# Streaming 128 columns instead of 32 through the products of a triangular inverse

## The chip, the cores and the metric

The kernel runs on one core of a Trainium2 chip. The metric is the device time of one execution in microseconds. Engines are named as the profile names them: PE (TensorE matmuls), PEld (TensorE weight loads), DVE (VectorE), ACT (ScalarE), POOL (GpSimd) and SP (SyncE).

## The reference

Two blocks follow each other. The first is a recurrence over 768 steps, for 4 batch elements and 8 heads of width 40. Its output, regrouped as 3072 rows of 320, goes to a router that sends each row to one of 8 experts (320 to 1024 to 320), all in fp32.

```python
for t in range(S):
    y[:, :, t] = np.einsum('bhd,bhde->bhe', rt, state)
    Sa = np.einsum('bhde,bhe->bhd', state, at)
    state_decay = state * wt[:, :, None, :] - np.einsum('bhd,bhe->bhde', Sa, bt)
    state = state_decay + np.einsum('bhd,bhe->bhde', vt, kt)
...
expert_idx = np.argmax(logits, axis=1)
for e in range(E):
    h = np.maximum(x[mask] @ w1[e], 0.0)
    out[mask] = gate_w[mask, None] * (h @ w2[e])
```

## The kernel before

The recurrence is done in chunks of 32 steps. A tile holds four chunks of one batch element on the 128 partitions, for all 8 heads side by side; there are 24 tiles (6 tiles of 128 steps by 4 batch elements). For each chunk and head the kernel needs the inverse of a 32x32 triangular matrix. Because a tile has four chunks on 128 partitions, the matrices between steps are 128x128 and block diagonal, and one matmul per head handles four chunks at once.

Two functions share the work of a tile. `prepare` (line 192) does everything that needs no state, in parts divided by `yield`; `advance` (line 322) takes the four chunks one after the other through the state. The main loop (lines 447 to 454) traces `advance` of tile g and, at each of its yields, two parts of `prepare` of tile g+1. So the inverse of the next tile lies in the code between the chunks of this one. The order in which each engine gets its instructions is then set by the framework's scheduler, which reorders traced instructions by priority and by its own costs, allots buffers, and puts in all semaphores; that is why the rows below show PE's groups interleaved more finely than the code.

The steps of `prepare` that matter, in order:

- the products of decays (DVE scans at lines 202 and 205) and four sets of transposes on PE (line 237: `ln`, `an`, `kn`, `bn`, 40 rows by 40 columns each);
- `between` (line 242): the products `ne`, `ge`, `fe` (line 248), 40 rows deep, 128 columns streamed, evacuated with a mask by DVE (line 251);
- the inverse. It grows from blocks of 1 step to blocks of 32. The first level needs no product (line 292); the four others (lines 294 to 305) each do, for all 8 heads: transpose the present inverse `xt` in blocks on DVE (`turned`, line 281), spread it into the block diagonal `xe` on POOL (line 270), multiply `w = ne' xt` on PE (line 298), copy it to `ws` on ACT (line 300), multiply `x = xe' ws` on PE (line 303), and write part of the result into `xt` under a mask on DVE (line 304). `xt` and `ws` hold 8 heads of 32 columns, so a matmul streams 32 columns for one head;
- `te`, the block diagonal of the inverse (line 270 from line 306), then `gv` (line 312, 40 columns streamed) and `pt` (line 321, 128 rows deep, 128 columns streamed, 40 columns of weights).

`advance` has the first products of the tile (`u_ps` at line 332 and `y_ps` at line 337), per chunk the small matmuls at lines 349, 357, 362, 374 and 378 (32 or 40 rows deep, 40 columns) with DVE's updates of the state, and behind the chunks `ut` (387), `he` (248), `y_ps` (391), the row's logits (`lg_ps`, 408) and its gate. An fp32 matmul stands in the trace as two passes, each with a weight load of its own, so 8 heads make 16 passes. The transposes at line 237 are one pass each.

PSUM has eight banks; the pool `mmp` (line 99) gives five of them in turn to everything that asks for `bank(...)`: `w_ps` and `x_ps` take one each at every level. Three more hold `u`, `y` and `s`.

After the recurrence, some 2200 us into the span, the rows are sorted by expert and the experts run (lines 573 to 675): matmuls 128 rows deep that stream 512 (line 618) and 320 columns (line 645).

Of the kernel before, what the change touches and what calls it, by code (L numbers as in the profile page):

```python
# [14 lines left out]
AX = mybir.AxisListType  # L15
PSUM = bass.MemoryType.PSUM
CMAGIC = 12582912.0
# keeps a square root's argument in range; its root is lost in the 1e-6 that is added
TINY = 1e-30
P = 128  # L20
L = 32
# [3 lines left out]
def bc(ap, shape, axis):  # L25
    return ap.unsqueeze(axis).to_broadcast(shape)
# [3 lines left out]
def kernel(  # L30
# [12 lines left out]
    moe_w2: bass.AP,  # L43
    out: bass.AP,
):
    """RWKV-7 state recurrence in chunks of L steps, then top-1 routed experts.

    With lam_t the product of a chunk's decays before step t, per channel e,
        at = a lam_t,  kt = k / lam_(t+1),  bt = b / lam_(t+1)
        U  = (I + tril(at bt'))^-1 (at S' + tril(at kt') V)  # L50
        y  = lam (r S + tril(r V') kt - tril(r U') bt)
        S <- (S + V' kt - U' bt) lam_L
    where S is the state at the chunk's start and tril is strict.  A tile holds four chunks of
    one batch element on 128 partitions, so that matrices between steps are block diagonal.
    The kernel carries -U.  The inverse grows from blocks of one step to blocks of L steps:
    the off-diagonal block of a pair of inverted blocks X is that of X N X.
    """
    nc = tc.nc
    B, NT, D, H, _ = rT.shape
    S = NT * P  # L60
    N = B * S
# [33 lines left out]
    with ExitStack() as attn:  # L95
        cst = attn.enter_context(tc.tile_pool(name="cst", bufs=1))
        one = attn.enter_context(tc.tile_pool(name="one", bufs=1))
        two = attn.enter_context(tc.tile_pool(name="two", bufs=2))
# [3 lines left out]
        def bank(name):  # L102
            return mmp.tile([P, 512], FP32, tag="mm", name=name)

# [1 line left out]
        blk = cst.tile([P, P], FP32, name="blk")  # L106
        nc.vector.memset(blk, 0.0)
        for c in range(NCK):
# [28 lines left out]
        for j in range(L.bit_length() - 1):  # L137
            m = cst.tile([P, L], I32, name=f"level{j}")
# [7 lines left out]
        first = cst.tile([D, W1C], FP32, name="first")  # L146
# [2 lines left out]
        decay = cst.tile([D, W1C], FP32, name="decay")  # L149
        nc.vector.memset(decay[:, 0 :: L + 1], 0.0)  # L150

# [1 line left out]
        emb = two.tile([P, XW], FP32, tag="xr", name="emb")[0:E, 0:DM]  # L153
        nc.sync.dma_start(out=emb, in_=moe_expert_emb)
        tau = cst.tile([E, 1], FP32, name="tau")
# [15 lines left out]
        def h3(t):  # L171
            return t[:, 0:DM].rearrange("p (h d) -> p h d", h=H)

        def half(t):
            return t.rearrange("p (h x) -> p h x", h=4)

        state = {}
# [12 lines left out]
            loaded[g] = d  # L190

        def prepare(g, d):
            """Everything of a tile that needs no state, in parts."""
            d.update(loaded.pop(g))
            ck = "p (x t) -> p x t"

            # products of decays: before a step, and after it to the chunk's end
            body = decay[:, 0 : W1C - 1].rearrange(ck, t=L + 1)
            nc.scalar.copy(body[:, :, 1:], d["w"].rearrange("p h (c t) -> p (h c) t", t=L))
            lam = one.tile([D, W1C], FP32, tag="lam", name="lam")  # L200
            suf = one.tile([D, W1C], FP32, tag="suf", name="suf")
            nc.vector.tensor_tensor_scan(
                lam, decay, first, initial=0.0, op0=ALU.mult, op1=ALU.add
# [26 lines left out]
            nc.gpsimd.tensor_tensor(d["k"], d["k"], d["w"], ALU.mult)  # L230
            nc.gpsimd.tensor_tensor(d["b"], d["b"], d["w"], ALU.mult)

            # steps on partitions
            for nm, src in (("ln", lx), ("an", d["a"]), ("kn", d["k"]), ("bn", d["b"])):
                ps = h3(bank(f"{nm}_ps"))
                for h in range(H):
# [5 lines left out]
            def between(nm, lhs, rhs, mask, pool):  # L242
                t = pool.tile([P, H, P], FP32, tag=nm, name=nm)
                for q in range(2):
                    ps = half(bank(f"{nm}_ps"))
                    for j in range(4):
                        h = 4 * q + j
                        nc.tensor.matmul(  # L248
                            ps[:, j], lhsT=lhs[:, h], rhs=rhs[:, h], start=True, stop=True
                        )  # L250
                    nc.vector.tensor_tensor(
                        t[:, 4 * q : 4 * q + 4], ps, bc(mask, [P, 4, P], 1), ALU.mult
                    )
                return t

            d["between"] = between
            ne = between("ne", d["a"], d["b"], nlower, one)
# [7 lines left out]
            def c3(t):  # L265
                return t[:, 0 : H * L].rearrange("p (h j) -> p h j", h=H)

            def block_diagonal(x, nm):
                t = one.tile([P, H, P], FP32, tag=nm, name=nm)
                nc.gpsimd.tensor_tensor(  # L270
                    t.rearrange("p h (c j) -> p h c j", c=NCK),
                    bc(x, [P, H, NCK, L], 2),
                    bc(blk.rearrange("p (c j) -> p c j", c=NCK), [P, H, NCK, L], 1),
                    ALU.mult,
                )
                return t

            # inverse of I - N, transposed
            def turned(x):
                t = two.tile([P, H, L], FP32, tag="xn", name="xn")  # L280
                nc.vector.transpose(  # L281
                    t.rearrange("p h j -> p (h j)"), x.rearrange("p h j -> p (h j)")
                )
                return t

            xt = two.tile([P, H, L], FP32, tag="xt", name="xt")
# [6 lines left out]
            yield  # L293
            for m in levels[1:]:
                xe = block_diagonal(turned(xt), "xe")
                ps = c3(bank("w_ps"))
                for h in range(H):
                    nc.tensor.matmul(ps[:, h], lhsT=ne[:, h], rhs=xt[:, h], start=True, stop=True)  # L298
                ws = two.tile([P, H, L], FP32, tag="ws", name="ws")
                nc.scalar.copy(ws, ps)  # L300
                ps = c3(bank("x_ps"))
                for h in range(H):
                    nc.tensor.matmul(ps[:, h], lhsT=xe[:, h], rhs=ws[:, h], start=True, stop=True)  # L303
                nc.vector.copy_predicated(xt, bc(m, [P, H, L], 1), ps)  # L304
                yield
            te = block_diagonal(xt, "te")

# [9 lines left out]
            for q in range(2):  # L317
                ps = half(bank("pt_ps"))
                for j in range(4):
                    h = 4 * q + j  # L320
# [3 lines left out]
                nc.scalar.copy(pt[:, 4 * q : 4 * q + 4], ps[0:D])  # L324

        def advance(g, d):
            """Four chunks through the state; the tile's rows of x, their gates and experts."""
            b, i = groups[g]
            u_ps = h3(acc.tile([P, 512], FP32, tag="u", name="u_ps"))
            y_ps = h3(acc.tile([P, 512], FP32, tag="y", name="y_ps"))  # L330
            for h in range(H):
                nc.tensor.matmul(
                    u_ps[:, h], lhsT=d["te"][:, h], rhs=d["gv"][:, h],
                    start=(h == 0), stop=False, skip_group_check=True,
                )
            for h in range(H):
                nc.tensor.matmul(
                    y_ps[:, h], lhsT=d["fe"][:, h], rhs=d["kn"][:, h],
                    start=(h == 0), stop=False, skip_group_check=True,
# [3 lines left out]
            for c in range(NCK):  # L343
                r0 = L * c
                rows = slice(r0, r0 + L)
                last = i == NT - 1 and c == NCK - 1
                st = state[b]
                for h in range(H):
                    nc.tensor.matmul(  # L349
                        u_ps[rows, h], lhsT=d["pt"][:, h, rows], rhs=st[:, h],  # L350
                        start=False, stop=True, skip_group_check=True,
                    )
                nc.vector.tensor_scalar(un[rows], u_ps[rows], -1.0, None, ALU.mult)
                if not last:
                    s_ps = h3(acc.tile([P, 512], FP32, tag="s", name="s_ps"))[0:D]
                    for h in range(H):
                        nc.tensor.matmul(  # L357
                            s_ps[:, h], lhsT=d["kn"][rows, h], rhs=d["vn"][rows, h],
                            start=(h == 0), stop=False, skip_group_check=True,
                        )  # L360
                    for h in range(H):
                        nc.tensor.matmul(  # L362
                            s_ps[:, h], lhsT=d["bn"][rows, h], rhs=un[rows, h],
                            start=False, stop=True, skip_group_check=True,
# [12 lines left out]
                for h in range(H):  # L377
                    nc.tensor.matmul(  # L378
                        y_ps[rows, h], lhsT=d["r"][:, h, rows], rhs=sn[:, h],
                        start=False, stop=False, skip_group_check=True,  # L380
# [3 lines left out]
            for q in range(2):  # L384
                ps = half(bank("ut_ps"))
# [4 lines left out]
            for h in range(H):  # L390
                nc.tensor.matmul(
                    y_ps[:, h], lhsT=he[:, h], rhs=d["bn"][:, h],
                    start=False, stop=True, skip_group_check=True,
                )
            xr = two.tile([P, XW], FP32, tag="xr", name="xr")
            x = xr[:, 0:DM]
            nc.vector.tensor_tensor(h3(xr), y_ps, d["ln"], ALU.mult)

            # logits times the row's norm, the first of the largest, the gate
            xt_ps = bank("xt_ps")  # L400
            for j, (k0, kn) in enumerate(KC):
                nc.tensor.transpose(xt_ps[0:kn, j * P : j * P + P], xr[:, k0 : k0 + kn], ident)
# [4 lines left out]
            for j, (_, kn) in enumerate(KC):  # L407
                nc.tensor.matmul(
                    lg_ps, lhsT=xs[0:kn, j], rhs=embT[0:kn, j],
                    start=(j == 0), stop=(j == len(KC) - 1),  # L410
# [34 lines left out]
        for _ in prepare(0, ready):  # L445
            pass
        for g in range(NG):
            now, ready = ready, {}
            ahead = prepare(g + 1, ready) if g + 1 < NG else iter(())
            for _ in advance(g, now):  # L450
                next(ahead, None)
                next(ahead, None)
            for _ in ahead:
                pass
            if g % 2 == 1 and g // 2 < E:
                load_w2(g // 2)
# [7 lines left out]
        )  # L464
        nc.scalar.dma_start(out=w1_sb[0 : KC[2][1], e, 2], in_=moe_w1[e, 2 * P : DM])

# [1 line left out]
    with ExitStack() as rt:  # L468
        rp = rt.enter_context(tc.tile_pool(name="rp", bufs=1))
        rps = rt.enter_context(tc.tile_pool(name="rps", bufs=1, space=PSUM))  # L470
# [15 lines left out]
        for e in range(1, E):  # L486
# [3 lines left out]
        before = rp.tile([P, P], FP32, name="before")  # L490
# [7 lines left out]
            rk, lhsT=ones, rhs=cumx.rearrange("p s e -> p (s e)"),  # L498
            start=True, stop=False, skip_group_check=True,
# [3 lines left out]
            start=False, stop=True, skip_group_check=True,  # L503
# [16 lines left out]
        off = rp.tile([P, E], FP32, name="off")  # L520
# [11 lines left out]
        nc.vector.scalar_tensor_tensor(  # L532
            out=lo, in0=bk, scalar=-float(P), in1=dest, op0=ALU.mult, op1=ALU.add
        )
        # tokens as two parts under 64, which bfloat16 holds exactly, as it does 0 and 1
        shp = [P, NSLOT, NBLK]
        bm = rp.tile(shp, FP32, name="bm")
        nc.vector.tensor_tensor(bm, bc(io_p[:, 0:NBLK], shp, 1), bc(bk, shp, 2), ALU.is_equal)
# [5 lines left out]
        q = NSLOT // 4  # L544
# [5 lines left out]
        for s in range(NSLOT):  # L550
            nc.tensor.matmul(
                inv, lhsT=oh[:, s], rhs=rr[:, s].rearrange("p t k -> p (t k)"),
                start=(s == 0), stop=(s == NSLOT - 1),
# [16 lines left out]
        nc.vector.tensor_reduce(n1.unsqueeze(2), cm, axis=AX.X, op=ALU.add)  # L570
        nc.vector.tensor_scalar(eblk, n1, -1.0, None, ALU.add)

# [1 line left out]
    fw = ctx.enter_context(tc.tile_pool(name="fw", bufs=2))  # L574
    xins = [fw.tile([P, XW], FP32, name=f"xin{j}", bufs=1) for j in range(XBUF)]
    for t in xins:
# [140 lines left out]
```

## Time and profile before

| | |
|---|---|
| runs | 2609.22 us and 8315.88 us |
| median of the two | 5462.55 us |
| span of the profiled execution | 2610.3 us |
| the run that agrees with that span | 2609.22 us |
| PE busy | 2519.8 us, 97% |
| PEld busy | 2211.9 us, 85% |
| DVE, ACT, POOL busy | 692.9, 375.9, 542.8 us |

The profile is of one execution. Busy time is the time in which an engine had an instruction in flight. Since matmuls are pipelined, a group of n passes is best priced by the start of the next group less its own start, over n: the mean ns that the table of lines gives for one pass includes the pass before it. The granted clock is TensorE's, as a share of full speed: 1.00 is 2.4 GHz and 0.50 is 1.2 GHz.

### The profile page before, as it was taken

What the parts mean: (1) busy time and instruction counts of PE and PEld (TensorE: products, weight loads), DVE (VectorE), ACT (ScalarE), POOL (GpSimd) and SP (SyncE); (2) the same over time, 40 slices, a digit from 0 to 9 for tenths busy, and PEclk for the clock granted to TensorE, in tenths of its full rate; (3) what the DMA queues carried; (4) which work ended last, traced back from release to release, by engine and by line L of the source; (5) the groups of instructions that cost most, each with busy time, mean ns of one, the idle gap of its engine ahead of it and who ended that gap; (6) DMA issues with size and microseconds to landing.
All of it is one profiled execution on the core that took longest, in us unless ns stands there. A gap on an engine that the chain in (4) does not pass through costs nothing. (4 is left out here: it accounts for less than half of the span.)

```text
span 2610.3 us, 35907 instructions
## 1 busy us (share of the span) xinstructions
PE 2519.8 (97%) x15728; PEld 2211.9 (85%) x15728; DVE 692.9 (27%) x1374; ACT 375.9 (14%) x769; POOL 542.8 (21%) x336
## 2 busy tenths in 40 slices
PE   6999999999999999999999999999999998699998
PEld 5999999999999999999999999999999997255554
DVE  4232232233223223312322331332233122211111
ACT  1011111011111101111110111111011102011111
POOL 3122212212211221221122122212211210211111
PEclk9655555555555555555555555555555555799999
DMA  6000000000000000000000000000000001400000
GB/s 199 11 21 9 16 19 13 14 16 21 9 16 19 12 15 16 21 9 16 19 13 14 16 21 9 16 19 13 13 19 19 6 4 33 155 26 28 23 21 6
DMA packets 28411, 62.65 MB, mean 24 GB/s; under 512 B 4052, under 2 KB 18398, under 8 KB 28256
## 3 DMA queue, kind: packets, MB, share of 16 engines
q1 hardware_dynamic: 16320, 39.88, 5.0%
q10 hardware_dynamic: 8960, 12.58, 1.6%
q0 software_dynamic: 2976, 7.89, 1.0%
q8 instruction: 126, 2.06, 0.3%
q14 instruction: 29, 0.24, 0.0%
HBM read 53.60 MB, written 9.02 MB: 24 GB/s over the span
## 5 line engine op out<-in xcount | busy, mean ns | idle before, releaser
L270 POOL TENSOR_TENSOR xe<-xn,blk 128x1024 f32<-128x1024 f32 x96 | 226.9, 2364 | 1194.9 <-DVE xn L281 1011.3
L298 PE MATMUL w_ps<-xt,ne 128*128 128x32 f32 x1536 | 352.4, 403 | 3.2 <-DVE xt L304 3.2
L303 PE MATMUL x_ps<-ws,xe 128*128 128x32 f32 x1536 | 346.9, 402 | 8.1 <-ACT ws L300 7.3
L303 PEld LDWEIGHTS x_ps<-ws,xe 128*128 128x128 f32 x1536 | 334.7, 330 | 16.8 <-issue 7.4
L298 PEld LDWEIGHTS w_ps<-xt,ne 128*128 128x128 f32 x1536 | 336.4, 329 | 13.8 <-DVE xt L304 4.0
L618 PE MATMUL h_ps<-w_sb,xT 128*128 x372 | 184.6, 622 | 8.0 <-DMA w_sb<-in_moe_w_dram 8.0
L618 PEld LDWEIGHTS h_ps<-w_sb,xT 128*128 128x128 f32 x372 | 63.1, 189 | 113.7 <-issue 109.1
L304 DVE COPY_PREDICATED xt<-level,x_ps 128x256 f32<-128x256 int32 x96 | 42.4, 442 | 418.3 <-PE x_ps L303 418.3
L357 PE MATMUL s_ps<-vn,kn 32*40 32x40 f32 x1472 | 142.6, 265 | 0.0
L367 DVE TENSOR_TENSOR st<-s_ps,st 40x320 f32<-40x320 f32 x92 | 44.4, 483 | 367.0 <-PE s_ps L362 367.0
L300 ACT COPY ws<-w_ps 128x256 f32<-128x256 f32 x96 | 35.7, 372 | 728.4 <-PE w_ps L298 728.4
L645 PE MATMUL y_ps<-w_sb,hT 128*128 x496 | 138.8, 433 | 0.0
L376 ACT COPY sn<-sn_ps 40x320 f32<-40x320 f32 x96 | 40.2, 419 | 613.7 <-PE sn_ps L374 613.7
L357 PEld LDWEIGHTS s_ps<-vn,kn 32*40 32x40 f32 x1472 | 112.3, 171 | 19.0 <-issue 5.4
L349 PE MATMUL u_ps<-st,pt 40*32 40x40 f32 x1536 | 125.9, 264 | 0.0
L378 PE MATMUL y_ps<-sn,in_r 40*32 40x40 f32 x1536 | 122.6, 265 | 0.0
L378 PEld LDWEIGHTS y_ps<-sn,in_r 40*32 40x32 f32 x1536 | 106.6, 163 | 17.7 <-issue 13.2
L645 PEld LDWEIGHTS y_ps<-w_sb,hT 128*128 128x128 f32 x496 | 91.7, 190 | 34.2
L349 PEld LDWEIGHTS u_ps<-st,pt 40*32 40x32 f32 x1536 | 106.9, 162 | 16.2 <-issue 9.4
L362 PE MATMUL s_ps<-un,bn 32*40 32x40 f32 x1472 | 116.9, 263 | 0.4 <-DVE gs L434 0.4
L362 PEld LDWEIGHTS s_ps<-un,bn 32*40 32x40 f32 x1472 | 105.9, 176 | 7.1 <-issue 4.5
L248 PE MATMUL fe_ps<-in_r,in_v 40*128 40x128 f32 x384 | 105.7, 444 | 0.0
(180 smaller groups left out, 3301.4 us busy)
## 6 DMA issues: line engine op xcount, KB each, us to landing
w_sb<-in_moe_w_dram ACTq DMA_DIRECT2D x8, 1280.0 KB
w_sb<-in_moe_w_dram SPq DMA_DIRECT2D x8, 1024.0 KB
x_rows<-xr SPq DMA_DIRECT2D x24, 160.5 KB
in_w<-in_wT_dram SPq DMA_DIRECT2D x24, 160.0 KB
in_a<-in_aT_dram SPq DMA_DIRECT2D x24, 160.0 KB
in_k<-in_kT_dram SPq DMA_DIRECT2D x24, 160.0 KB
in_b<-in_bT_dram SPq DMA_DIRECT2D x24, 160.0 KB
in_v<-in_vT_dram SPq DMA_DIRECT2D x24, 160.0 KB
```

Source lines behind the costliest of these rows:

```text
L248: nc.tensor.matmul(ps[:, j], lhsT=lhs[:, h], rhs=rhs[:, h], start=True, stop=True)
L270: nc.gpsimd.tensor_tensor(t.rearrange("p h (c j) -> p h c j", c=NCK), bc(x, [P, H, NCK, L], 2), bc(blk.rearrange("p (c j) -> p c j", c=NCK ...
L298: nc.tensor.matmul(ps[:, h], lhsT=ne[:, h], rhs=xt[:, h], start=True, stop=True)
L303: nc.tensor.matmul(ps[:, h], lhsT=xe[:, h], rhs=ws[:, h], start=True, stop=True)
L304: nc.vector.copy_predicated(xt, bc(m, [P, H, L], 1), ps)
L349: nc.tensor.matmul(u_ps[rows, h], lhsT=d["pt"][:, h, rows], rhs=st[:, h], start=False, stop=True, skip_group_check=True,)
L357: nc.tensor.matmul(s_ps[:, h], lhsT=d["kn"][rows, h], rhs=d["vn"][rows, h], start=(h == 0), stop=False, skip_group_check=True,)
L362: nc.tensor.matmul(s_ps[:, h], lhsT=d["bn"][rows, h], rhs=un[rows, h], start=False, stop=True, skip_group_check=True,)
L367: nc.vector.tensor_tensor(new, s_ps, st, ALU.add)
L378: nc.tensor.matmul(y_ps[rows, h], lhsT=d["r"][:, h, rows], rhs=sn[:, h], start=False, stop=False, skip_group_check=True,)
L618: nc.tensor.matmul(ps, lhsT=d["xT"][0:kn, c], rhs=w1f[0:kn, ds(ek * (len(KC) * F) + c * F + q * 512, 512)], start=(c == 0), stop=(c == len ...
L645: nc.tensor.matmul(ps, lhsT=d["hT"][:, c], rhs=w2f[:, ds(d["ek"] * (FC * DM) + c * DM, DM)], start=(c == 0), stop=(c == FC - 1),)
```

## The change

At each of the four levels that multiply, the 8 heads are taken in two groups of four. The streamed operand of each matmul is now the 32 columns of all four heads of the group (128 columns), for `w` and for `x`. A head's matmul gives the product of its own weights with all four heads' columns, fills a quarter of a bank, and of its 128 columns the 32 of its own head are kept. So a level has as many matmuls, weights and passes as before, each with four times the columns; it takes four PSUM banks in place of two; and the one ACT copy and the one masked DVE copy of 256 columns become eight of each with 32 columns, four behind each bank. The masks, the transposes, `xe` and the results are unchanged. Comments and the docstring are blanked, which leaves the line numbers ahead of the loop as they were.

```diff
             for m in levels[1:]:
                 xe = block_diagonal(turned(xt), "xe")
-                ps = c3(bank("w_ps"))
-                for h in range(H):
-                    nc.tensor.matmul(ps[:, h], lhsT=ne[:, h], rhs=xt[:, h], start=True, stop=True)
                 ws = two.tile([P, H, L], FP32, tag="ws", name="ws")
-                nc.scalar.copy(ws, ps)
-                ps = c3(bank("x_ps"))
-                for h in range(H):
-                    nc.tensor.matmul(ps[:, h], lhsT=xe[:, h], rhs=ws[:, h], start=True, stop=True)
-                nc.vector.copy_predicated(xt, bc(m, [P, H, L], 1), ps)
+                wide = "p (h x) -> p h x"
+                for q in range(2):
+                    ps = bank("w_ps")
+                    rhs = xt[:, 4 * q : 4 * q + 4].rearrange("p h j -> p (h j)")
+                    for j in range(4):
+                        nc.tensor.matmul(
+                            ps[:, P * j : P * j + P], lhsT=ne[:, 4 * q + j], rhs=rhs,
+                            start=True, stop=True,
+                        )
+                    for j in range(4):
+                        o = P * j + L * j
+                        nc.scalar.copy(ws[:, 4 * q + j], ps[:, o : o + L])
+                for q in range(2):
+                    ps = bank("x_ps")
+                    rhs = ws[:, 4 * q : 4 * q + 4].rearrange("p h j -> p (h j)")
+                    for j in range(4):
+                        nc.tensor.matmul(
+                            ps[:, P * j : P * j + P], lhsT=xe[:, 4 * q + j], rhs=rhs,
+                            start=True, stop=True,
+                        )
+                    for j in range(4):
+                        o = P * j + L * j
+                        nc.vector.copy_predicated(xt[:, 4 * q + j], m, ps[:, o : o + L])
                 yield
```

## Rows read from the trace of the kernel before

**Rows 1.** The page: span, busy times, granted clock in 40 equal slices.
```profile
span 2610.3 us, 35907 instructions
...
PE 2519.8 (97%) x15728; PEld 2211.9 (85%) x15728; DVE 692.9 (27%) x1374; ACT 375.9 (14%) x769; POOL 542.8 (21%) x336
...
PEclk9655555555555555555555555555555555799999
```

**Rows 2.** Stages: window, length, busy PE PEld DVE ACT POOL, clock, DMA share, GB/s.
```profile
300.00:1000.00 700.00, 693.78 (x4643) 648.55 (x4643) 192.87 (x366) 105.33 (x221) 152.69 (x79) 0.50 0.05 15
...
2300.00:2500.00 200.00, 200.00 (x681) 107.14 (x680) 33.54 (x86) 30.41 (x53) 35.82 (x35) 1.00 0.08 26
```

**Rows 3.** Groups of instructions by line and shape, whole span.
```profile
L298 PE MATMUL w_ps<-xt,ne 128*128 128x32 f32 x1536 | 352.4, 403 | 3.2 <-DVE xt L304 3.2
L303 PE MATMUL x_ps<-ws,xe 128*128 128x32 f32 x1536 | 346.9, 402 | 8.1 <-ACT ws L300 7.3 <-POOL xe L270 0.8
...
L270 POOL TENSOR_TENSOR xe<-xn,blk 128x1024 f32<-128x1024 f32 x96 | 226.9, 2364 | 1194.9 <-DVE xn L281 1011.3 <-DVE lam_l L210 183.6
...
L312 PE MATMUL gv_ps<-vn,ge 128*128 128x40 f32 x384 | 87.8, 415 | 0.0
```

**Rows 4.** Timeline of PE around one level: start us, us, engine, line, names, passes.
```profile
1001.36 3.62 PE L248 MATMUL ge_ps<-in_a,in_k 40*128 40x128 f32 x16
1004.90 0.74 PE L349 MATMUL u_ps<-st,pt 40*32 40x40 f32 x8
...
1013.85 1.27 PE L349 MATMUL u_ps<-st,pt 40*32 40x40 f32 x16
1015.06 0.35 PE L357 MATMUL s_ps<-vn,kn 32*40 32x40 f32 x2
...
1015.98 3.62 PE L298 MATMUL w_ps<-xt,ne 128*128 128x32 f32 x16
1019.53 1.28 PE L362 MATMUL s_ps<-un,bn 32*40 32x40 f32 x16
...
1021.95 3.62 PE L303 MATMUL x_ps<-ws,xe 128*128 128x32 f32 x16
```

**Rows 5.** Stretches of 2 us with a raised clock: window, length, PE busy, clock.
```profile
172.00:174.00 2.00, 2.00 (x21) 0.82 0.00 0
174.00:176.00 2.00, 2.00 (x33) 1.00 0.00 0
176.00:178.00 2.00, 2.00 (x12) 0.53 0.24 82
...
2176.00:2178.00 2.00, 2.00 (x27) 0.91 0.00 0
```

**Rows 6.** Timeline of PE where the clock rises, and of a tile without.
```profile
81.09 1.98 PE L332 MATMUL u_ps<-gv,te 128*128 128x40 f32 x16
83.00 0.69 PE L237 MATMUL ln_ps<-ident,lx 40*128 40x40 f32 x8
...
992.92 2.88 PE L321 MATMUL pt_ps<-te,an 128*40 128x128 f32 x14
995.73 0.68 PE L237 MATMUL ln_ps<-ident,lx 40*128 40x40 f32 x8
996.25 0.67 PE L237 MATMUL an_ps<-ident,in_a 40*128 40x40 f32 x8
...
1085.37 1.07 PE L237 MATMUL ln_ps<-ident,lx 40*128 40x40 f32 x8
1086.25 1.05 PE L237 MATMUL an_ps<-ident,in_a 40*128 40x40 f32 x8
```

**Rows 7.** Groups by line and shape: evacuations from PSUM.
```profile
L304 DVE COPY_PREDICATED xt<-level,x_ps 128x256 f32<-128x256 int32 x96 | 42.4, 442 | 418.3 <-PE x_ps L303 418.3
...
L300 ACT COPY ws<-w_ps 128x256 f32<-128x256 f32 x96 | 35.7, 372 | 728.4 <-PE w_ps L298 728.4
...
L314 ACT COPY gv<-gv_ps 128x320 f32<-128x320 f32 x24 | 10.2, 426 | 83.6 <-PE gv_ps L312 83.6
```

## The prediction

> **What bounds the kernel now.** I read the page first: TensorE is busy for 97% of the span, no other engine for more than 27%, and the line of granted clocks stands at 5 tenths from the third slice to the thirty-third [rows 1]. The table of stages says the same without rounding: from 300 to 1000 us PE is busy for 693.78 of 700 us at a clock of 0.50, which is the lower of its two levels, 1.2 GHz; the experts, from 2300 to 2500 us, run at 1.00, 2.4 GHz [rows 2]. So the recurrence, some 2200 us, is bound by PE, and by a PE at half speed. What a change is worth here is read in PE time, and a change of clock is worth more than anything that another engine can give.
>
> The groups by line come next [rows 3]. The two products of the inverse, lines 298 and 303, are its largest: 1536 passes each, 352.4 and 346.9 us, together 27% of the span. PE sits idle ahead of them for 3.2 and 8.1 us in all, so their inputs nearly always lie ready.
>
> Then the timeline, for the price of one pass [rows 4]. The 16 passes of `w` start at 1015.98 and the next group at 1019.53: 222 ns a pass for 32 streamed columns. The 16 passes of `ge` start at 1001.36 and the next group at 1004.90: 221 ns for 128 streamed columns. Both have weights of 128 columns. A small pass, 40 rows with weights of 32 columns and 40 streamed, takes 76 ns (1013.85 to 1015.06 for 16). So the weight load sets the pace of `w`, and the columns flow beside the next load: 96 more columns cost nothing in the nearest row. The Trainium skill ("TensorE: Matmul & The Clock Gate", section "Back-to-back issue gap") speaks against this: it gives the gap between single matmuls as the streamed columns over the clock, so that four times the columns would be four times the gap, 107 in place of 27 ns at the lower clock. By that alone the 3072 passes would grow by an estimated 3072 x 80 ns = 246 us; the two equal rows disagree with it for weights of this width.
>
> Last, where the clock rises within the recurrence. Stretches of 2 us show seven spells above 0.50, near 172, 630, 994, 1268, 1632, 2086 and 2176 us, of which the first and last stand in [rows 5]; each lasts about 3.4 us (in the first 0.82, 1.00 and 0.53, so 1.3, 2 and 0.1 us at the upper level). In each of them the engine had just done `pt`. In the third, 14 passes of it, 128 rows deep and 128 columns wide, run from 992.92 to 995.73, and the transposes behind them take 65 ns each (995.73 to 996.25 for 8), against 110 ns in a tile without the spell (1085.37 to 1086.25) [rows 6]. There is an eighth at 81 us behind the first tile's `pt`: `u_ps` takes 119 ns a pass there (81.09 to 83.00 for 16), though it has the same weights as the passes of 222 ns. (The recorded clock of 1.00 ahead of that is not borne out: passes have the slow pace until then.) So 8 of 24 stretches of `pt` raised the clock. Neither `ge` and its kin (128 columns, 40 rows deep) nor `gv` (128 rows, 40 columns streamed, [rows 3]), nor the present `w` and `x` (128 rows, 32 columns) was ever followed by a rise of its own. All the while PE was as good as always busy.
>
> **The change part by part.** *The passes.* As many as before, 2 x 1536, with the same weights. At the lower clock 128 columns cost between nothing (`ge`) and, if each pass were 10 ns longer because its stream is now as long as its load, 3072 x 10 ns = 31 us. I take 5 us, near `ge`. A gain is excluded, since the loads are the same.
>
> *The clock.* After the change every stretch of `w` or `x` is 16 passes, 128 rows deep and 128 columns wide: what `pt` is, but for weights of 128 columns in place of 40, and the experts, which hold 1.00, have such weights. There are 8 such stretches per tile (4 levels, `w` and `x`) where there was one of `pt`. If each raises the clock as often as `pt` did, that is 8/3 = 2.7 spells per tile. The bounds are none and one for each stretch, 8; most `pt` stretches are cut in two by the logits' passes and the `w` stretch in [rows 4] is whole, so I go a little up, to 3. The price of one spell of 3.4 us is bounded by two rows [rows 4, 6]: with transposes 3.4 x (110/65 - 1) = 2.35 us of work gained, with passes of 128 weight columns 3.4 x (222/119 - 1) = 2.9 us. What follows `w` is mostly small passes, nearer to the transposes: 2.3 us. Sum: 3 x 2.3 x 24 = 166 us.
>
> *The evacuations.* ACT's copy takes 372 ns for 256 columns and 426 ns for 320 [rows 7], so 0.84 ns a column and some 157 ns fixed: 184 ns for 32 columns. Eight take 1.47 us, 1.1 us more per level, 96 x 1.1 = 106 us on an engine that is busy for 375.9. The masked copy on DVE has only its 442 ns; with a like fixed part one of 32 columns takes some 0.2 us, eight 1.6 us, 111 us more on an engine busy for 692.9. Neither becomes the bound. What counts is the tail between a stretch of PE and the next. Four of the eight copies wait for the first bank alone and run beside the second half of the stretch; behind `w` four copies of 0.18 us stand in place of one of 0.37, and the first half of `x` needs only the earlier four. Behind `x` four masked copies, 0.8 us, stand in place of 0.44, and then come the transpose and POOL's 2.36 us [rows 3] as before. This tail has small matmuls of the present tile to hide it, at 1019.53 for one [rows 4]; it shows where there are none, in the first tile, and where PE gets ahead. Between nothing and 0.45 us at each of 96 levels, 43 us: I take 10.
>
> *The banks.* A level takes four of the five shared banks in turn in place of two. A bank is held longer only by its four short copies, and PE has 3.5 us of work in the other bank of the pair. I cost it at nothing; if the cover is gone, it is part of the 43 us above.
>
> The sum: 5 + 10 - 166 = -151 us. The profiled span of 2610.3 us agrees with the run of 2609.22; the median of 5462.55 is the midpoint of that run and one of 8315.88, a time that neither had and that nothing in the profile accounts for. The forecast is made against 2609.22: 2609 - 151 = 2458 us.
>
> **The rivals.** *The clock stays up through the levels.* If the scheduler puts `x` right behind `w`, or if a raised clock needs less to stay than to rise, the whole stretch of the levels, 1014 to 1058 of a tile's 90 us, runs at 1.00. At 119/222 and 65/110 of the pace that is 44 x 0.43 = 19 us per tile: 2609 - 24 x 19 + 15 = 2168. Against it: every spell seen ended after some 3.4 us, and at 2.4 GHz a stretch of 16 passes is over in 2 us.
>
> *The clock does not rise.* `gv`, as deep and with the same 128 weight columns, never raised it; perhaps the long load is what keeps `w` from it, not the columns. Then only the costs remain: 2609 + 15 = 2624. A rule of the Trainium skill leads there too (the same page, section "What's actually happening"): the clock is set by how busy PE has recently been. By it the recurrence, with PE 99% busy, would be at full clock already and wider streams could give nothing. The 0.50 beside 693.78 of 700 us disagrees with that plain reading.
>
> *The evacuations decide* (slower). If the copies do not overlap with the other half, and PE finds nothing else to do, a level gets longer by all that they add, 1.1 + 1.16 = 2.3 us, 217 us in 96 levels: 2609 + 217 + 5 - 166 = 2665. It decides from 166/96 = 1.7 us per level on. For it speaks that `x` already waits for `ws` in places (7.3 us, [rows 3]); against it, that those waits are 11 us in 192 stretches.
>
> *Load and stream in sequence* (slower). If a stream 128 rows deep does not fit beside the load, a pass gains what 128 columns take alone: some 222 ns of a `ge` pass less the 76 ns of a small one, 146 ns, or 449 us in all: 2609 + 449 - 166 = 2892. It decides from 166 us/3072 = 54 ns per pass on. `ge` speaks against it. The page's estimate of 246 us from above, put in its place, would give 2609 + 246 - 166 = 2689.
>
> **How the numbers follow.** The forecast has 0.72, the clock that stays up 0.10, the clock that does not rise 0.10, the evacuations 0.06, the sequence 0.02. Five spells per tile with the sum's costs make 2609 - 276 + 15 = 2348, two with both costs at their upper bound 2609 - 110 + 74 = 2573: that is the likeliest case's own range. Below I stop at 2340; above I reach to 2625, to take in the clock that does not rise. The other three cases, 0.18, are left out. Some 2% is what a measurement of this kernel can tell from no change, so faster means under 2557: 0.69 of the first case and all of the second, 0.79. Within 2% are 0.03 of the first and the third case, 0.13. Slower is 0.08.
>
> **What would show it.** Right: in stretches of 2 us, spells at 1.00 in the middle of the tiles, behind `w` or `x`, three or so per tile; groups of 16 passes with 128 columns that take 3.5 to 3.7 us at 0.50 and near 2 us at 1.00; the mean clock of 300 to 1000 us near 0.56 (3 x 3.4 of 84 us); PE still busy above 97%. Wrong: a clock of 0.50 throughout; passes of `w` above 235 ns at the lower clock; idle time of PE ahead of lines 298 and 303 in tens of us, released by ACT or DVE. If whole tiles stand at 1.00, the first rival was right.

## The result and the profile after

The changed kernel takes 2189.22 us (2181.05 and 2197.39), 0.8385 of the time before, with an interval of 0.8249 to 0.8522. Run again beside its experiments it took 2189.42 us against 2612.88, a ratio of 0.8354 (0.8317 to 0.8392); the ratios are taken over runs in the faster of two states, and one repeat of 2210.57 us was in the slower. So it is faster by a sixth, 420 us, where 151 us were forecast; the time of 2189 us lies below the range of 2340 to 2625 us. All ratios below are against the kernel before on the same chip, whose runs there lay between 2606 and 2618 us.

The page of the changed kernel, against [rows 1]: span, busy times, and the granted clock in 40 equal slices.

```profile
span 2195.7 us, 37553 instructions
...
PE 2063.8 (94%) x15728; PEld 1765.9 (80%) x15728; DVE 837.1 (38%) x2046; ACT 428.0 (19%) x1441; POOL 581.9 (26%) x336
...
PEclk9677656657776677766776577657666657999999
```

PE has the same 15728 passes and is busy for 456 us less; its share fell to 94%, where above 97% was expected, since it now waits (below). The clock line explains how: 6 and 7 tenths through the recurrence in place of 5 (0.70 from 300 to 1000 us, where 0.56 was forecast). DVE has 144 us more and ACT 52, neither near a bound.

The groups by line, against [rows 3, 7]; the change moves line 298 to 302, 303 to 313, 300 to 308 and 304 to 319, and what follows by 15.

```profile
L270 POOL TENSOR_TENSOR xe<-xn,blk 128x1024 f32<-128x1024 f32 x96 | 261.9, 2729 | 876.0 <-DVE xn L281 858.2 <-DVE lam_l L210 17.8
L302 PE MATMUL w_ps<-xt,ne 128*128 128x128 f32 x1536 | 258.0, 324 | 4.4 <-DVE xt L319 4.4
...
L313 PE MATMUL x_ps<-ws,xe 128*128 128x128 f32 x1536 | 221.6, 305 | 46.5 <-POOL xe L270 46.5
...
L383 DVE TENSOR_TENSOR st<-st,lam_l 40x320 f32<-40x320 f32 x92 | 113.5, 1234 | 2.3
...
L319 DVE COPY_PREDICATED xt<-level,x_ps 128x32 f32<-128x32 int32 x768 | 93.5, 189 | 263.0 <-PE x_ps L313 262.9
...
L308 ACT COPY ws<-w_ps 128x32 f32<-128x32 f32 x768 | 87.1, 200 | 359.9 <-PE w_ps L302 359.6
```

`w` and `x` with four times the columns take 480 us in place of 699. A small masked copy costs 189 ns (some 200 were forecast), a small ACT copy 200 (184 were); four in a row overlap, so each engine has 51 us more of them, half of what was forecast. New is PE's wait ahead of `x`, 46.5 us for POOL, where 8.1 us for ACT and POOL stood before.

One tile by stages, the changed kernel: transposes to the first `w`, the levels to the end of the last `x`, and the rest to the next tile's transposes.

```profile
1018.00:1038.60 20.60, 20.60 (x178) 18.94 (x177) 11.11 (x17) 4.44 (x10) 0.00 (x0) 0.56 0.14 41
1038.60:1065.80 27.20, 25.80 (x259) 24.07 (x257) 12.37 (x39) 4.46 (x34) 11.31 (x4) 0.83 0.01 2
1065.80:1088.80 23.00, 22.41 (x178) 20.50 (x177) 8.84 (x21) 6.97 (x14) 10.65 (x6) 0.70 0.08 22
```

The same three stages of a tile before:

```profile
995.70:1016.00 20.30, 20.30 (x178) 18.53 (x177) 11.28 (x17) 3.88 (x9) 0.00 (x0) 0.57 0.14 41
1016.00:1057.80 41.80, 41.61 (x297) 39.89 (x297) 6.88 (x17) 3.37 (x7) 13.59 (x6) 0.50 0.02 5
1057.80:1085.40 27.60, 27.02 (x139) 24.57 (x138) 7.27 (x15) 6.00 (x12) 6.07 (x4) 0.50 0.04 12
```

This is where the time went: the three stages of this tile are 18.9 us shorter, the levels by 14.6, at a clock of 0.83 in place of 0.50, and what follows them by 4.6, at 0.70 for 0.50 (the first is 0.3 longer). Stretches of 2 us (window, length, PE busy, clock) show one long spell in this tile, from the end of the first level's `x` into the passes behind `he`:

```profile
1046.00:1048.00 2.00, 2.00 (x12) 0.54 0.00 0
...
1050.00:1052.00 2.00, 1.33 (x27) 1.00 0.00 0
...
1062.00:1064.00 2.00, 1.26 (x25) 1.00 0.00 0
...
1074.00:1076.00 2.00, 2.00 (x18) 0.78 0.38 90
```

Nothing like the 3.4 us of [rows 5]: the clock is up from 1047.8 to 1075.1, 27.3 us. It outlasts stretches in which PE is idle for a third of the time. Over the recurrence there is one long spell per tile, of 17 to 27 us, and 17 short ones of 3.4 us as before, mostly behind `pt`; from 100 us on to the experts 628 us are spent at 1.00, where it was 24.

The timeline of PE in that spell (start, us, engine, line, names, passes, idle before and its releaser), against [rows 4]:

```profile
1043.70 1.70 PE L302 MATMUL w_ps<-xt,ne 128*128 128x128 f32 x7
1045.19 3.21 PE L313 MATMUL x_ps<-ws,xe 128*128 128x128 f32 x16
1048.24 1.96 PE L302 MATMUL w_ps<-xt,ne 128*128 128x128 f32 x16
1050.14 0.76 PE L364 MATMUL u_ps<-st,pt 40*32 40x40 f32 x16
1050.83 0.49 PE L372 MATMUL s_ps<-vn,kn 32*40 32x40 f32 x8
1051.98 2.05 PE L313 MATMUL x_ps<-ws,xe 128*128 128x128 f32 x16 [0.67 <-POOL xe L270]
1053.97 0.49 PE L372 MATMUL s_ps<-vn,kn 32*40 32x40 f32 x8
1054.30 0.78 PE L377 MATMUL s_ps<-un,bn 32*40 32x40 f32 x16
1055.01 0.46 PE L389 MATMUL sn_ps<-ident,st 40*40 40x40 f32 x8
...
1067.21 1.75 PE L327 MATMUL gv_ps<-vn,ge 128*128 128x40 f32 x14
...
1069.83 1.04 PE L402 MATMUL ut_ps<-ident,un 128*40 128x128 f32 x8
...
1071.40 2.05 PE L248 MATMUL he_ps<-in_r,ut 40*128 40x128 f32 x16
```

The scheduler's order is new too: the end of the first `w`, the first `x` and the second `w` follow one another without a break. A wide pass takes 119 ns at the upper clock (1048.24 to 1050.14 for 16), a small one 43 ns (1050.14 to 1050.83), against 222 and 76.

### The profile page after: what moved, and what is told of

Its sections match the earlier page's. It is cut to its first block, busy times and chain, and to the rows that moved or that the text cites. A ratio compares the mean times of both kernels' runs of the same rounds, so it can differ in the third digit from the quotient of the medians.

```text
span 2195.7 us, 37553 instructions
## 1 busy us (share of the span) xinstructions
PE 2063.8 (94%) x15728; PEld 1765.9 (80%) x15728; DVE 837.1 (38%) x2046; ACT 428.0 (19%) x1441; POOL 581.9 (26%) x336
## 5 line engine op out<-in xcount | busy, mean ns | idle before, releaser
L270 POOL TENSOR_TENSOR xe<-xn,blk 128x1024 f32<-128x1024 f32 x96 | 261.9, 2729 | 876.0 <-DVE xn L281 858.2
L313 PE MATMUL x_ps<-ws,xe 128*128 128x128 f32 x1536 | 221.6, 305 | 46.5 <-POOL xe L270 46.5
L302 PE MATMUL w_ps<-xt,ne 128*128 128x128 f32 x1536 | 258.0, 324 | 4.4 <-DVE xt L319 4.4
L313 PEld LDWEIGHTS x_ps<-ws,xe 128*128 128x128 f32 x1536 | 208.9, 218 | 53.4 <-POOL xe L270 53.1
L302 PEld LDWEIGHTS w_ps<-xt,ne 128*128 128x128 f32 x1536 | 225.4, 227 | 13.2 <-issue 4.6
L319 DVE COPY_PREDICATED xt<-level,x_ps 128x32 f32<-128x32 int32 x768 | 93.5, 189 | 263.0 <-PE x_ps L313 262.9
L308 ACT COPY ws<-w_ps 128x32 f32<-128x32 f32 x768 | 87.1, 200 | 359.9 <-PE w_ps L302 359.6
L383 DVE TENSOR_TENSOR st<-st,lam_l 40x320 f32<-40x320 f32 x92 | 113.5, 1234 | 2.3
L372 PE MATMUL s_ps<-vn,kn 32*40 32x40 f32 x1472 | 105.9, 235 | 0.0
L372 PEld LDWEIGHTS s_ps<-vn,kn 32*40 32x40 f32 x1472 | 87.3, 145 | 15.5 <-issue 5.6
```

The source lines that it names most:

```text
L270: nc.gpsimd.tensor_tensor(t.rearrange("p h (c j) -> p h c j", c=NCK), bc(x, [P, H, NCK, L], 2), bc(blk.rearrange("p (c j) -> p c j", c=NCK ...
L302: nc.tensor.matmul(ps[:, P * j : P * j + P], lhsT=ne[:, 4 * q + j], rhs=rhs, start=True, stop=True,)
L313: nc.tensor.matmul(ps[:, P * j : P * j + P], lhsT=xe[:, 4 * q + j], rhs=rhs, start=True, stop=True,)
L319: nc.vector.copy_predicated(xt[:, 4 * q + j], m, ps[:, o : o + L])
L372: nc.tensor.matmul(s_ps[:, h], lhsT=d["kn"][rows, h], rhs=d["vn"][rows, h], start=(h == 0), stop=False, skip_group_check=True,)
L383: nc.vector.tensor_tensor(new, new, bc(d["lamL"][:, :, c], [D, H, D], 2), ALU.mult)
```

## The experiments

**Own columns only.** The banks and the sixteen small evacuations of the change, but each matmul streams its own head's 32 columns (`x` likewise).

```diff
-ps[:, P * j : P * j + P], lhsT=ne[:, 4 * q + j], rhs=rhs,
+ps[:, P * j + L * j : P * j + L * j + L], lhsT=ne[:, 4 * q + j], rhs=xt[:, 4 * q + j],
```

> Same four banks and sixteen small evacuations per level as the changed kernel, but each matmul streams only the 32 columns of its own head. If the raised clock, brought by the 128 columns, is the whole gain: the clock stands at 0.50 through the recurrence again, the mean over the span is near 0.59, and the time is 2609 to 2660 us, what lies above 2609 being the price of the evacuations and banks (0 to 43 us were forecast). If the gain came from the banks, the smaller copies or the order of instructions that they bring: about 2190 us at a clock of 0.50.

It took 2638.32 us, a ratio of 1.0096 (1.008 to 1.0113), in the first theory's range, with the recurrence at half speed, as a stretch of it shows:

```profile
1000.00:1500.00 500.00, 499.05 (x3314) 459.46 (x3314) 166.10 (x408) 86.47 (x301) 101.09 (x52) 0.51 0.06 16
```

(The mean clock of this profile, 0.646, says nothing: 1.00 stands in its records for the first 370 us, which the passes do not bear out.) So without the columns the change loses 25 us, the price of its banks, copies and order, and the gain is gone: banks and small copies do not bring it. Since the order is not the changed kernel's, this tells the columns apart from the evacuations, not from the order.

**One wide level.** 128 columns at the first, or at the last of the four levels, the others as before the change, for `w` and in the same way for `x`. The second kernel has `levels[-1]` in the first line.

```diff
+if m is levels[1]:
     for q in range(2):
         ps = bank("w_ps")
...
+else:
+    ps = c3(bank("w_ps"))
+    for h in range(H):
+        nc.tensor.matmul(ps[:, h], lhsT=ne[:, h], rhs=xt[:, h], start=True, stop=True)
+    nc.scalar.copy(ws, ps)
...
```

> 128 columns in the first of the four levels alone, the others as before the change. If a raised clock needs less to stay than to rise: one rise per tile behind the first level's w and x, and the clock then stays up through the narrow levels, 15 us or more per tile, mean clock of the recurrence 0.60 or more, time 2230 to 2400 us. If the wide stretches themselves hold it up: the clock falls one spell of 3.4 us behind the last wide pass, some 3.4 to 7 us per tile, and the time is 2500 to 2570 us.

> 128 columns in the last of the four levels alone. If a raised clock needs less to stay than to rise: it rises behind the last level and stays up through gv, ut and he as it does in the changed kernel, 7 to 17 us per tile, time 2350 to 2480 us. If the wide stretches hold it up: one spell of 3.4 us, at most 7, per tile, and 2500 to 2570 us. Either way dearer than the first level alone, if what follows the rise is what pays.

The first level alone took 2551.7 us (ratio 0.9766, 0.9747 to 0.9786), in the range of the second theory; most of its spells last 6.8 us. Its PE and its clock behind the wide level:

```profile
997.72 2.52 PE L320 MATMUL x_ps<-ws,xe 128*128 128x128 f32 x16
1000.08 0.98 PE L313 MATMUL w_ps<-xt,ne 128*128 128x32 f32 x8
1000.99 0.54 PE L376 MATMUL u_ps<-st,pt 40*32 40x40 f32 x10
```

```profile
1000.00:1002.00 2.00, 2.00 (x29) 1.00 0.00 0
...
1004.00:1006.00 2.00, 1.14 (x26) 0.93 0.00 0
1006.00:1008.00 2.00, 2.00 (x11) 0.50 0.03 8
```

Narrow `w` passes and small ones do not hold the clock for long. (In this tile PE also sat idle for 0.86 us just ahead of the fall; the lone stretches below fall with PE never idle.) The last level alone took 2411.89 us, and 2456.09 in the run that was profiled; both are in the range of the first theory, and its spells of up to 10 us reach through `gv`, `ut` and `he`. It was expected to be dearer than the first level alone and is cheaper by some 100 to 140 us; why is not shown. So neither theory holds in its plain form: a raised clock outlasts the wide passes of the levels by some microseconds, and for how long differs with what comes behind them.

**Lone stretches.** `x` wide, `w` as before the change.

> 128 columns in x alone, w as before the change, so that no two wide stretches follow one another: the forecast's own picture of lone stretches of 16 passes. If a lone stretch raises the clock as often as pt did and the spell ends after 3.4 us, as the forecast had it: about 4/3 spells per tile from x, 3.4 us each, time 2530 to 2580 us. If lone stretches can hold the clock as well: spells of 7 us and more and less than 2480 us. If only stretches in unbroken sequence raise it: as before the change, 2610 to 2650 us.

This took 2543.19 us, 0.9734 (0.9689 to 0.9779), in the first theory's range. It has two spells in most tiles, nearly all of 3.4 us, in the tile looked at each behind an `x`; here PE is busy throughout:

```profile
1088.97 3.78 PE L306 MATMUL x_ps<-ws,xe 128*128 128x128 f32 x16
1092.68 0.72 PE L382 MATMUL sn_ps<-ident,st 40*40 40x40 f32 x8
```

```profile
1092.00:1094.00 2.00, 2.00 (x17) 0.60 0.00 0
1094.00:1096.00 2.00, 2.00 (x24) 1.00 0.03 8
1096.00:1098.00 2.00, 2.00 (x48) 0.76 0.00 0
```

**Fewer evacuations.** One strided copy per bank on ACT and one masked copy on DVE in place of four and four.

```diff
-for j in range(4):
-    o = P * j + L * j
-    nc.scalar.copy(ws[:, 4 * q + j], ps[:, o : o + L])
+own = bass.AP(tensor=ps.tensor, offset=ps.offset, ap=[ps.ap[0], [P + L, 4], [1, L]])
+nc.scalar.copy(ws[:, 4 * q : 4 * q + 4], own)
```

> 128 columns as in the changed kernel, but the four kept blocks of a bank leave in one strided copy on ACT and one masked copy on DVE, so 2 and 2 per level in place of 8 and 8. If the tail of small copies lies on the chain that PE now waits for (46.5 us ahead of x, released by POOL's block diagonal): 0.2 to 0.4 us less per level, PE's wait ahead of x 10 to 30 us, time 2150 to 2180 us. If the tail is hidden: 2189 us within 0.5%.

Neither theory held: it took 2368.99 us, 0.907 (0.9055 to 0.9086), 180 us slower than the changed kernel with less work for ACT and DVE, and PE's wait ahead of `x` is 74.1 us. PE's order and clock in one tile point to why:

```profile
993.13 0.33 PE L362 MATMUL u_ps<-st,pt 40*32 40x40 f32 x4
994.81 2.05 PE L312 MATMUL x_ps<-ws,xe 128*128 128x128 f32 x16 [1.35 <-POOL xe L270]
996.79 0.61 PE L362 MATMUL u_ps<-st,pt 40*32 40x40 f32 x12
997.33 0.80 PE L370 MATMUL s_ps<-vn,kn 32*40 32x40 f32 x16
998.06 0.32 PE L387 MATMUL sn_ps<-ident,st 40*40 40x40 f32 x4
998.31 0.80 PE L375 MATMUL s_ps<-un,bn 32*40 32x40 f32 x16
999.04 0.32 PE L387 MATMUL sn_ps<-ident,st 40*40 40x40 f32 x4
```

```profile
998.00:1000.00 2.00, 2.00 (x34) 1.00 0.00 0
1000.00:1002.00 2.00, 2.00 (x25) 0.78 0.04 8
```

In the changed kernel 24 small passes stand ahead of the second `x`, in its wait for POOL, and 32 behind it. Here 4 stand ahead, the wait is longer, and 52 small passes lie in one piece behind; the clock falls in the next `w`, in the middle of the levels.

**Shorter waits for POOL.** The block diagonal in two halves of four heads, both on POOL, or the first on DVE (as in the diff); then also `gv` on 128 columns, with and without the halves.

```diff
+for q, eng in enumerate((nc.vector, nc.gpsimd)):
+    r = slice(4 * q, 4 * q + 4)
+    eng.tensor_tensor(
+        t[:, r].rearrange("p h (c j) -> p h c j", c=NCK),
+        bc(x[:, r], [P, 4, NCK, L], 2),
...
...
-nc.tensor.matmul(gv_ps[:, h], lhsT=ge[:, h], rhs=d["vn"][:, h], start=True, stop=True)
+nc.tensor.matmul(ps[:, j], lhsT=ge[:, 4 * q + j], rhs=vf[:, c0 : c0 + P], start=True, stop=True)
```

> The changed kernel with POOL's block diagonal in two instructions of four heads each, so that the first half of x can start some 1.2 us earlier. If PE's wait for POOL (46.5 us ahead of x) only costs its own length: the wait falls to 20 us or less, time 2140 to 2175 us. If what counts is how long small passes and waits part one wide group from the next: longer spells at the upper clock (27 us and more per tile) and 2050 to 2140 us, or, should the scheduler collect the small passes in one place as with the single copies, shorter spells and more than 2250 us.

> The changed kernel with the first half of the block diagonal on DVE and the second on POOL, side by side. Same theories as for the halves on POOL alone: PE's wait ahead of x near nothing, worth 40 to 50 us by its own length, 2140 to 2160 us; if the spells at the upper clock also lengthen, 2000 to 2120 us.

> The last kernel, and gv streams 128 columns too (of which a head keeps 40), behind the last level. If wide streams close behind one another are what holds the clock: the spell runs on through gv, ut and he, 30 us or more per tile, and the time is 30 to 100 us below the kernel without it. If gv is too short to matter or its place in the order shifts: within 30 us of it.

> The changed kernel with gv on 128 columns and nothing else, to part the two edits of the 2111 us kernel; the block diagonal on POOL whole, as in the changed kernel. If the wide gv made that gain (it was 175 us against the DVE half alone): 2080 to 2150 us. If it was the order of instructions that the scheduler makes of the two together: 2170 us or more.

The halves on POOL took 2302.5 us (0.8813, 0.8777 to 0.8848), the third case of their expectation; the wait that they were to cut did not fall (51.1 us), and the spells are of some 20 us, in some tiles two of 10. With one half on DVE PE's wait ahead of `x` fell to 9.6 us, and the time rose to 2286.8 us (0.8753, 0.8664 to 0.8841), outside both ranges: its spells are nearly all of 17 us. With `gv` wide as well: 2111.24 us (0.8081, 0.8053 to 0.8108), the fastest yet, 176 us below the kernel without it where 30 to 100 were expected. The wide `gv` on the changed kernel alone: 2185.95 us (0.8362, 0.8323 to 0.8401), no difference. So the wide `gv` gains nothing by itself; the two edits together have spells of 17 to 27 us and 8.9 us of waits. What makes the 176 us is not shown, for two things differ at once. In the tiles looked at small passes no longer part the first `w` from the first `x`, and the clock rises earlier; and where it fell within the narrow `gv` with the half on DVE alone, it stays up through the wide one.

**Passes that nobody reads.** Four wide passes among each chunk's small ones, added to the changed kernel, and to the 2111 us kernel.

```diff
+fl = bank("fl_ps")
+for j in range(2):
+    nc.tensor.matmul(fl[:, P * j : P * j + P], lhsT=blk, rhs=blk, start=True, stop=True)
```

> The changed kernel plus two matmuls per chunk whose product nobody reads (128 rows, 128 columns, weights of 128 columns: 4 passes), put among the small passes of the state; 92 chunks, 368 passes, which alone cost 44 us at the upper clock (119 ns) and 82 us at the lower (222 ns). If the time is set by PE's work at whatever clock the levels get, and the stretches between them have no part in it: 2230 to 2270 us. If the upper clock is lost because small passes lie too long without a wide group among them: the spells get longer, 27 us or more in nearly every tile, and the added work pays for itself in part or whole, 2080 to 2200 us.

> The kernel with half of the block diagonal on DVE and gv on 128 columns (2111 us), plus the same unread matmuls. If unread work can only cost: 2150 to 2195 us. If it holds the upper clock for longer: more than 0.75 mean clock and 1980 to 2110 us, the best of all so far.

On the changed kernel it took 2325.27 us (0.8895, 0.8876 to 0.8913), dearer than both theories had it: the passes take 90 us of PE, in the tile looked at half of them at the lower clock, and the spells of 24 us end ahead of `he`. On the other kernel it took 2160.58 us (0.8269, 0.8251 to 0.8286): the time at 1.00 does grow, from 618 to 689 us, and the added 91 us of PE cost more than that brings. Unread work to hold the clock does not pay here.

**The order alone, and the evacuations alone.** Two kernels to part what the last ones left mixed. The first is the changed kernel, with the small passes `u` and the first half of `s` of two chunks held behind the `x` traced last. The second is the 2111 us kernel with one strided ACT copy per bank (the edit above); the kernel without it ran beside it.

```diff
+after_x = c > 1 and last_x[0] is not None and g + 1 < NG
+with tc.issue_after(last_x[0].ins) if after_x else ExitStack():
     for h in range(H):
         nc.tensor.matmul(
             u_ps[rows, h], lhsT=d["pt"][:, h, rows], rhs=st[:, h],
...
```

> The changed kernel with the same passes, banks and evacuations, but the small passes of the third and fourth chunk (u and the first half of s) may be issued only behind the x of the second and fourth product level, as the scheduler put them with single copies. If the order alone decides how long the clock stays up (small passes ahead of x, in its wait for POOL, keep the stretch behind x short): spells of 10 us, two to a tile, or shorter ones in other ways, clock of the recurrence 0.65 or less, time 2290 to 2400 us. If the small copies were what kept the clock up, not the order: 2190 to 2250 us, the difference being PE's longer wait.

> The fastest kernel with one strided ACT copy per bank of w in place of four; its order on PE is the same in the tiles looked at. If the order decides and the copies have no part in it: within 1% of 2111 us, a little less for the shorter tail (0.2 us at 96 levels, up to 20 us). If single copies shorten the spells by themselves, as the 2369 us of the kernel with single copies might be read: 2200 us or more.

> The fastest kernel so far once more, for its interval: 2105 to 2118 us.

The order alone took 2394.13 us, 0.9151 (0.9125 to 0.9177), as the first theory had it. Its PE and its clock show the same break as the kernel with single copies:

```profile
1010.28 2.05 PE L314 MATMUL x_ps<-ws,xe 128*128 128x128 f32 x16 [1.77 <-POOL xe L271]
1012.26 0.76 PE L367 MATMUL u_ps<-st,pt 40*32 40x40 f32 x16
```

```profile
1014.00:1016.00 2.00, 2.00 (x36) 0.86 0.00 0
1016.00:1018.00 2.00, 2.00 (x14) 0.50 0.00 0
```

The waits ahead of `x` grew to 94.8 us, so 48 of the 205 us lost are waiting; most of the rest is the clock, 0.62 from 300 to 1000 us in place of 0.70. The longer waits could themselves be what brings the clock down, but in the tile above it stayed at 1.00 from 1008 to 1010 us, with PE busy for 0.51 of the 2 us, and fell behind the small passes, with PE busy throughout; and the half on DVE, with hardly a wait, has short spells too. The evacuations alone took 2104.22 us (0.8049, 0.8017 to 0.8082) against 2103.55 (0.8051, 0.8031 to 0.8071, just under the expected range), no difference. So a change of order alone can cost as much as the single copies did, and single copies on ACT cost nothing where the order stays. That the 180 us came through the order that the scheduler made is the reading that fits both; the single masked copy on DVE was not tried alone.

The last control, the changed kernel again, gave its 2189.42 us.

> The changed kernel once more, beside the three below on one chip: 2175 to 2205 us, as in its first runs.

## Why the prediction was wrong, and where it was right

Right: what bounds the kernel, that the clock is what the change moves, and the way it goes. The term of the passes holds: 16 wide passes of `x` at the lower clock take 223 ns each where a `w` follows (1079.62 to 1083.19 in the kernel with lone stretches) and 232 where `sn` does (1088.97 to 1092.68, shown above), 1 to 10 ns more than the 222 of narrow ones. That is 3 to 31 us for all 3072, so the 5 us taken lie at the low end, and load and stream do not run in sequence. The evacuations' engine time, half of the forecast, and their place off the path hold; own columns alone cost 25 us, where 10 were taken for evacuations and banks and 43 were the bound.

The step that failed is the price of one spell. The forecast took "each lasts about 3.4 us" from what followed `pt`, and gave every rise that price: three spells, 10.2 us per tile at the upper clock. Measured are 628 us in some 23 tiles, 27 us per tile. The count of spells was even too high: 40 in 23 tiles, 1.7 per tile, of which one is long. The gain per microsecond at 1.00 was sized a little low: 2.3/3.4 is 0.68, and the measured 415 us, with 25 us for the edits and 40 us of new waits added, over 604 us give 0.80. The lone stretches of `x` show that the forecast's own case exists, and gives 70 us. What the change made is another case: stretches that follow closely, the small passes among them spread out.

The first rival named that, "if the scheduler puts `x` right behind `w`, or if a raised clock needs less to stay than to rise", and priced it at 2168 us, 21 off; it was given 0.10. The evidence held against it, that every spell seen had ended after 3.4 us, was about what came next in those places: transposes 40 rows deep, and `ne`. It said nothing on what would follow a `w`. That the rival's time came so near is in part luck: it had the levels at 1.00 for all of their 44 us and nothing behind them, where the levels stand at 0.83 and a part of the gain lies behind them. Both halves of its condition are borne out. The order is the first half: with the small passes moved it is 2394 us. The second half is in the spell above: from the end of the last `x` at 1065.8 to `ut` at 1069.8 the clock stays up through `gv` with 40 columns and through `s`, `sn` and `y`, none of which was followed by a rise of its own before the change. (`ut` has the form of `pt`; it may help to hold the clock through `u` and `he`.)

The clock that does not rise and the sequence are refuted by the rows above. The slower rival of the evacuations met its own mechanism half way: PE now does wait, for POOL and not for the copies, 46.5 us. The Trainium skill ("TensorE: Matmul & The Clock Gate", section "What's actually happening") has the clock set by how busy PE has been; the plain reading of that stays contradicted: with own columns PE was busy for 499.05 of 500 us at 0.51.

Still open is what sets the end of each single spell. In the changed kernel the tiles whose spells begin at 413 and 488 us run the same passes in the same order through the levels, and the one spell is over within `gv` after 20 us, the other 7 us later. So the order is not all of it.

## What to carry to other kernels

Where PE is busy all the time at the lower clock and its weight loads set the pace, streaming more columns beside them can cost next to nothing and raise the clock; look first at which forms of pass the clock rose behind. Price the rise by what will follow it, not by the length of the spells that happen to be in the trace, and give the case in which it lasts its own full weight. Then keep the wide groups close: read the order that the scheduler made, since an edit that saves work or waits can lose more by collecting small passes in one place.

## What the runs showed that was not expected

Three edits that were to save work or waits cost time: single copies 180 us, halves on POOL 113, half on DVE 98, each against 2189 us (the halves on POOL did not even save the wait). And DVE and POOL hold each other up: the product of the state with its decays (line 383, 368 before) took 1234 ns in the mean where it had taken 479, 113.5 us in place of 44.1. Where it started beside POOL's block diagonal, it ended 0.35 us behind it, as in this pair of lines. The other way round, the first block diagonal of a tile takes 4.24 us beside DVE's scan of line 205, at 325.25 us for one, where the others take 2.36:

```profile
1055.28 2.37 POOL L270 TENSOR_TENSOR xe<-xn,blk 128x1024 f32<-128x1024 f32 x1 [3.35 <-DVE xn L281]
1055.63 2.37 DVE L383 TENSOR_TENSOR st<-st,lam_l 40x320 f32<-40x320 f32 x1
```

The best version found, half of the block diagonal on DVE and `gv` on 128 columns, takes 2103.55 us, 4% less than the changed kernel and 0.8051 of the time before.
